# The third chunk's product with w_out as seven block products, in a newly ordered list

## The chip, the cores and the metric

The kernel runs on one core of a Trainium2 chip. The metric is device time in microseconds of one execution; the time before is the median of three runs. The profile is one more execution, recorded by the hardware profiler. In it PE is TensorE (PEld its weight loads), DVE VectorE, ACT ScalarE, POOL GpSimd and SP SyncE, which here issues DMAs only.

## The reference

A causal linear attention with a decay per head, followed by a two-layer network with a leaky activation. Four batches, eight heads, 768 positions, head size 64; the network goes from 512 to 2048 and back to 512 for 3072 tokens.

```python
for b in range(S // 64):                       # blocks of 64 positions
    intra = (q_b @ k_b.T) * Dmask              # Dmask[i, j] = lam ** (i - j) for i >= j, else 0
    out_b = intra @ v_b + (q_b * lam_pow) @ kv_state
    kv_state = lam ** 64 * kv_state + (k_b * rev_pow).T @ v_b
x = out.transpose(0, 2, 1, 3).reshape(3072, 512)
h = x @ w_in                                   # 512 -> 2048
g = max(h, 0) + alpha * min(h, 0)
result = g @ w_out                             # 2048 -> 512, float32
```

## The kernel before, in words

**Chunks and units.** The 3072 tokens are six chunks `c` of 512: two batches (`bi`) times 256 positions. The attention of a chunk is done in four units (`bi`, half of the heads `hh`), numbered 0 to 23, so that unit `n` belongs to chunk `n // 4`. For a unit, `load` and `load16` bring q, k and v into SBUF, `cast` makes fp16 of q and k, `turn` with `turned` (on TensorE and a copy) or `turn_by_dma` (a transposing DMA on SyncE's queue, from unit 8 on) turns them, `key_decayed` and `decayed` scale k and q, and `spread` copies a state into the block layout RD. `cluster(old, new)` is TensorE's part: the scores of unit `new` and its state's update (tiles `s` and `acc`), and the outputs of unit `old`, whose scores `masked` has multiplied by the decay mask on VectorE. `state` carries the state on; `out_of` puts the unit's output into xT.

**The network.** `up(c, f, bi, slot)` multiplies a chunk by one of 16 blocks of 128 columns of w_in, four matmuls into a PSUM bank `slot` (tile `h_ps`); `bi=None` means all 512 tokens. `below` (ScalarE) makes the negative part `m`, `gate` (VectorE) writes G from `m` and `h_ps`. The bank is free for another `up` when its `gate` is done.

**The product with w_out.** There are two forms. Chunks 0 to 2 use `down(c, t, part)`: for each of four row tiles `t` 16 matmuls of 512 columns (tile `o_ps`), in parts of four, then `store`, a copy on ScalarE and a DMA on its queue. Chunks 3 to 5 use seven block products instead of eight: G is cut into rows `e` and block parity `r`, w_out into parity and column half. `product(c, k, bi)` is block product `k` for one half of the tokens, eight matmuls of 256 columns (tile `p_ps`). It needs sums of G's blocks (`SUM`, tile `gsum`; sum 3 is made in G itself) and of w_out's (`WS`, tile `wsum`, made by `weight_sum` and negated by `weight_less`). `taken` collects a product into the output tile (ScalarE copies for 1, 6, 7, 4; VectorE adds for 2, 5, 3), and SyncE stores it. A sum of G is made in halves `h`, either by `gate_sum` (an addition on VectorE or GpSimd) or by `gate_copied` and `gate_added`: a DMA on SyncE that copies the first addend, and a DMA on GpSimd's queue that adds the second one. In the list before, chunk 3 uses the DMAs, chunks 4 and 5 use `gate_sum` on VectorE.

**Order.** The scheduling is manual: every engine and every DMA queue executes its instructions in the order of one long list of calls at the end of the kernel, and waits where data or a buffer is not ready. The list is written out, call by call; its opening is common to both versions. The tables `PRODUCTS`, `WHEN` and the function `sums_in` above the list are not called by it. Buffers come from pools of fixed size (four for raw q, five for raw k, two output tiles), so a load or a first write may wait for the last reader of an older tile. The two G buffers alternate between chunks. `hold` writes one element of a raw tile, which makes a load wait for VectorE's place in the list. `fill` are matmuls whose results are not used.

Of the kernel before, what the change touches and what calls it, by code (L numbers as in the profile page):

```python
# [11 lines left out]
def kernel(  # L12
# [434 lines left out]
    G = {}  # L447
# [67 lines left out]
    SUM = {}  # L515
# [38 lines left out]
    def parts(c, k, h, where="q"):  # L554

        if k != 3 and (c, k) not in SUM:
            SUM[c, k] = late(where, "gsum")
        x = {n: SUM[c, n][:, ds(h * HJ, HJ)] for n in (1, 2, 4) if (c, n) in SUM}
        x[3] = block_of(c, 1, 0, h)
        a, b = {  # L560
            1: lambda: (x[3], block_of(c, 1, 1, h)),
            2: lambda: (block_of(c, 0, 0, h), x.get(1)),
            3: lambda: (x[3], block_of(c, 0, 0, h)),
            4: lambda: (block_of(c, 0, 1, h), x.get(2)),
        }[k]()
        return x[k], a, b

    def gate_sum(c, k, h, where="q", eng="V"):
        x, a, b = parts(c, k, h, where)
        engine(eng).tensor_tensor(out=x, in0=a, in1=b, op=ALU.add)  # L570
# [66 lines left out]
    def weight_less_of(c, k, h):  # L637
        weight_less(h)

    WHEN = {  # L640
        (3, 9): [(gate_copied, 1, 0), (gate_copied, 2, 0)],
        (3, 10): [(gate_added, 1, 0), (gate_added, 3, 0)],
        (3, 12): [(gate_copied, 4, 0)],
        (3, 13): [(gate_added, 2, 0)],
        (3, 14): [(weight_less_of, 2, 0)],
        (4, 0): [(weight_less_of, 2, 1), (gate_copied, 1, 1), (gate_copied, 2, 1), (gate_copied, 4, 1)],
        (4, 1): [(gate_added, 1, 1), (gate_added, 3, 1), (gate_added, 2, 1)],
        (4, 5): [(gate_added, 4, 0)],
        (4, 8): [(gate_added, 4, 1)],
    }  # L650

    def sums_in(x):

        if 17 <= x <= 20:
            for h in range(2):
                weight_sum((1, 2, 4, 3)[x - 17], h)
# [89 lines left out]
    state(1, 0)  # L746
    cast(4, "k", "A")
# [6 lines left out]
    masked(2, 1)  # L754
    turned(3, "A")
# [12 lines left out]
    load_win(3)  # L768
    hold("k", 2, 0)
    masked(3, 0)  # L770
    spread(3, 1, "A", True)
# [3 lines left out]
    cast(6, "q", "G")  # L775
    turn(4)
    turned(4, "V")
    cast(7, "q", "G")
    zeros(2, 0, "G")
    out_of(2, "A")  # L780
    spread(8, 0, "A")
    below(0, 2, 0)
    key_decayed(5, "G")
    fill(14, 0)
    state(3, 1)
    cluster(3, None)
# [19 lines left out]
    hold("k", 1, 1)  # L806
    gate(0, 6, None)
    gate(0, 5, None)
    state(4, 0)
    up(0, 4, None, 1)  # L810
    load("k", 1, 1)
    spread(4, 1, "V")
    below(0, 0, 1)
    up(0, 8, None, 2)
    gate(0, 0, 1)
    cast(5, "q", "V")
    load("k", 2, 0, ring=1)
    state(4, 1)
    up(0, 3, 1, 0)
    below(0, 4, None)  # L820
    load_wout(1)
    turn(5)
    below(0, 8, None)
    gate(0, 4, None)
    gate(0, 8, None)
    up(0, 7, None, 1)
    below(0, 3, 1)
    gate(0, 3, 1)
    masked(4, 1)
    up(0, 1, 1, 2)  # L830
    turned(5, "A")
    below(0, 1, 1)
    below(0, 7, None)
    masked(4, 0)
    load_wout(0)
    decayed(4, "G")
    gate(0, 1, 1)
    gate(0, 7, None)
    up(0, 9, None, 0)
    below(0, 9, None)  # L840
    cluster(4, 5)
    masked(5, 1)
    gate(0, 9, None)
    up(0, 11, None, 2)
    below(0, 11, None)
    gate(0, 11, None)
    state(5, 0)
    cast(6, "k", "G")
    zeros(3, 0)
    state(5, 1)  # L850
    up(0, 14, None, 1)
    load("q", 2, 0, ring=1)
    spread(5, 1, "A")
    below(0, 14, None)
    gate(0, 14, None)
    decayed(5, "G")
    up(0, 12, None, 0)
    up(0, 10, None, 2)
    masked(5, 0)
    below(0, 10, None)  # L860
    turn(6)
    up(0, 15, None, 1)
    out_of(4, "A")
    cluster(5, None)
    key_decayed(6, "G")
    gate(0, 10, None)
    cast(7, "k", "V")
    up(0, 13, None, 2)
    below(0, 12, None)
    turned(6, "V")  # L870
    below(0, 15, None)
    out_of(5, "A")
    turn(7)
    gate(0, 12, None)
    load_wout(2)
    up(1, 0, 0, 0)
    below(0, 13, None)
    cluster(None, 6)
    below(1, 0, 0)
    gate(0, 15, None)  # L880
    down(0, 2, 0, 1)
    gate(1, 0, 0)
    up(1, 2, 0, 0)
    gate(0, 13, None)
    below(1, 2, 0)
    hold("k", 2, 1)
    turned(7, "A")
# [3 lines left out]
    state(6, 0)  # L891
    load_wout(3)
    gate(1, 2, 0)
    decayed(6, "G")
    key_decayed(7, "V")
    below(1, 1, 0)
    gate(1, 1, 0)
    cast(9, "q", "V")
    decayed(7, "V")
    down(0, 1, 0, 0)  # L900
    spread(6, 1, "A")
    cast(9, "k", "V")
    down(0, 1, 1, 2)
    masked(6, 0)
    down(0, 0, 0, 2)
    down(0, 0, 1, 1)
    down(0, 0, 2, 1)
    state(6, 1)
    down(0, 1, 2, 2)
    cluster(6, 7)  # L910
    out_of(6, "A")
    down(0, 0, 3, 1)
    cast(8, "k", "V")
    load("k", 2, 1, ring=1)
    spread(9, 0, "V")
    load16("v", 2, 0)
    state(7, 0)
    cast(8, "q", "V")
    down(0, 2, 2, 2)
    down(0, 2, 3, 2)  # L920
    turn_by_dma(8)
    store(0, 0)
    spread(7, 1, "A")
    key_decayed(8, "G")
    store(0, 2)
    up(1, 3, 0, 2)
    below(1, 3, 0)
    masked(7, 0)
    masked(7, 1)
    state(7, 1)  # L930
    cast(10, "k", "V")
    weight_sum(1, 0)
    cluster(7, 8)
    masked(8, 1)
    key_decayed(9, "G")
    gate(1, 3, 0)
    down(0, 1, 3, 2)
    out_of(7, "A")
    up(1, 4, None, 1)
    turn_by_dma(9)  # L940
    store(0, 1)
    state(8, 0)
    below(1, 4, None)
    decayed(8, "G")
    load("q", 2, 1)
    key_decayed(10, "G")
    masked(8, 0)
    spread(8, 1, "G")
    up(1, 5, None, 0)
    state(8, 1)  # L950
    cluster(8, 9)
    below(1, 5, None)
    load("q", 3, 0)
    cast(11, "k", "V")
    up(1, 0, 1, 2)
    gate(1, 4, None)
    below(1, 0, 1)
    gate(1, 5, None)
    up(1, 1, 1, 1)
    below(1, 1, 1)  # L960
    gate(1, 0, 1)
    cast(10, "q", "A")
    up(1, 6, None, 0)
    cast(11, "q", "V")
    down(0, 3, 0, 2)
    gate(1, 1, 1)
    up(1, 7, None, 1)
    below(1, 6, None)
    load16("v", 3, 0)
    weight_sum(1, 1)  # L970
    down(0, 3, 1, 2)
    below(1, 7, None)
    gate(1, 6, None)
    masked(9, 1)
    load16("v", 2, 1)
    key_decayed(11, "V")
    up(1, 8, None, 0)
    state(9, 0)
    below(1, 8, None)
    down(0, 3, 2, 2)  # L980
    down(0, 3, 3, 2)
    turn_by_dma(10)
    cast(12, "q", "V")
    load("k", 3, 0)
    masked(9, 0)
    gate(1, 8, None)
    up(1, 11, None, 0)
    spread(9, 1, "A")
    decayed(9, "G")
    gate(1, 7, None)  # L990
    turn_by_dma(11)
    out_of(8, "V")
    store(0, 3)
    up(1, 10, None, 1)
    spread(13, 0, "A")
    decayed(10, "V")
    key_decayed(12, "G")
    below(1, 11, None)
    state(9, 1)
    below(1, 10, None)  # L1000
    cast(12, "k", "V")
    up(1, 13, None, 2)
    gate(1, 11, None)
    cluster(9, 10)
# [3 lines left out]
    load("k", 4, 0)  # L1008
    below(1, 9, None)
    up(1, 15, None, 1)  # L1010
    gate(1, 13, None)
    state(10, 0)
    load("k", 3, 1)
    load("q", 4, 0)
    gate(1, 9, None)
    below(1, 15, None)
    up(1, 12, None, 2)
    turn_by_dma(12)
    below(1, 12, None)
    up(1, 14, None, 0)  # L1020
    gate(1, 15, None)
    masked(10, 0)
    out_of(9, "A")
    cast(13, "q", "G")
    down(1, 0, 0, 1)
    below(1, 14, None)
    gate(1, 12, None)
    cast(13, "k", "G")
    down(1, 0, 1)
    decayed(11, "G")  # L1030
    up(1, 2, 1, 2)
    gate(1, 14, None)
    up(1, 3, 1, 0)
    down(1, 0, 2)
    spread(11, 0, "G")
    down(1, 0, 3)
    below(1, 3, 1)
    cast(14, "k", "G")
    key_decayed(13, "G")
    spread(10, 1, "V")  # L1040
    state(10, 1)
    spread(10, 0, "A")
    masked(10, 1)
    cluster(10, 11)
    spread(14, 0, "V")
    load("q", 3, 1)
    key_decayed(15, "G")
    gate(1, 3, 1)
    below(1, 2, 1)
    gate(1, 2, 1)  # L1050
    state(11, 0)
    cast(16, "k", "A")
    masked(11, 0)
    spread(11, 1, "V")
    state(11, 1)
# [36 lines left out]
    cast(17, "q", "G")
    store(1, 1)
# [482 lines left out]
```

## Time and profile before

| | |
|---|---|
| median of three runs | 213.61 us (213.57 to 213.88) |
| the profiled execution | 213.43 us, of which the span from first to last instruction is 211.6 us |
| TensorE busy | 200.9 us, 95% (2286 matmuls) |
| VectorE, ScalarE, GpSimd busy | 168.9, 112.7 and 83.5 us |
| mean granted TensorE clock | 1.00 |
| DMA | 33.54 MB, 158 GB/s over the span |

Busy is the time in which an engine executes; the ends of matmuls are modelled and overlap the next ones. Groups of instructions are named by the line of the kernel, the engine, the operation, the tile written and the tiles read, and the shape; then come the count, the busy time, the mean of one in ns, and the engine's idle time just before them with what ended it. The waits list names who waited for whom: total, times, longest. The chain of work that ended last is followed back from the end of the execution. "Landing" is the time from a DMA's issue to its arrival.

### The profile page before, as it was taken

The page shows a single profiled execution, that of the slowest core. Times are in us where ns is not written, and L with a number is a line of the kernel's source. Part 1 is how long each engine was busy: PE and PEld are TensorE (multiplying, and loading weights), DVE is VectorE, ACT ScalarE, POOL GpSimd, SP SyncE. Part 2 cuts the span into 40 slices and gives each one's busy share as a digit, 9 for nine tenths or more (in the row PEclk, how much of TensorE's full clock was granted, in tenths as well). Part 3 has the DMA queues.
Part 4 walks back from the last instruction along what each step waited for, and adds up shares of the span by engine and source line. Part 5 has one row for each costly group of instructions (what it writes and reads, how often), then busy time and mean ns, then how long its engine had stood idle before and what let it go on. Part 6 is the DMA issues. An engine that isn't in the chain of part 4 may idle for free.

```text
span 211.6 us, 5657 instructions
## 1 busy us (share of the span) xinstructions
PE 200.9 (95%) x2286; PEld 124.6 (59%) x2286; DVE 168.9 (80%) x347; ACT 112.7 (53%) x231; POOL 83.5 (39%) x122
## 2 busy tenths in 40 slices
PE   4798999999999999999999999999999999999992
PEld 4776555555555455455544545556666766766881
DVE  3799799999689994889988969999669778549731
ACT  3998576643647536455755556363464525354320
POOL 8989199170721570987960083213021000000000
PEclk9999999999999999999999999999999999999999
DMA  4999999998999999899999391867273211011213
GB/s 113 275 184 194 198 237 227 246 245 118 276 238 220 314 222 231 247 152 243 135 208 105 121 222 56 156 149 157 41 187 65 99 53 50 2 50 53 74 53 124
DMA packets 62443, 33.54 MB, mean 158 GB/s; under 512 B 34497, under 2 KB 58577, under 8 KB 62417
## 3 DMA queue, kind: packets, MB, share of 16 engines
q0 software_dynamic: 22096, 12.45, 41.1%
q1 hardware_dynamic: 38416, 17.57, 35.8%
q10 hardware_dynamic: 1904, 3.16, 4.4%
q8 instruction: 18, 0.29, 0.6%
q14 instruction: 9, 0.07, 0.1%
HBM read 27.28 MB, written 6.29 MB: 159 GB/s over the span
## 4 chain that ended last, share of the span: by engine, by line
PE 78%; ACT 9%; DVE 6%; DMA 4%; issue 2%; ACTq 0%; DVEq 0%; SPq 0%
PE h_ps L457 36%; PE p_ps L598 17%; PE o_ps L491 15%; PE s L362 3%; DVE g L481 3%; PE acc L374 2%; DMA qkT<-qk 2%; DMA lam_sb<-in_lam_dram 2%; ACT qkT L248 2%; PE acc L344 2%; ACT dmask L202 1%; DVE RD L250 1%; ACT qk L248 1%; PE acc L391 1%; DVE sm L403 1%
## 5 line engine op out<-in xcount | busy, mean ns | idle before, releaser
L457 PE MATMUL h_ps<-xT,w_in_sb 128*128 128x512 f16 (+1 forms) x416 | 92.8, 363 | 1.0 <-DVE g L481 0.6
L468 ACT ACTIVATE m<-h_ps 128x512 f32<-128x512 f32 (+1 forms) x104 | 57.5, 564 | 59.9 <-PE h_ps L457 55.0
L481 DVE SCALAR_TENSOR_TENSOR g<-m,oma,h_ps 128x512 f16<-128x512 f32 (+1 forms) x104 | 71.1, 702 | 19.3 <-ACT m L468 18.2
L457 PEld LDWEIGHTS <-w_in_sb 128*128 128x128 f16 x416 | 39.3, 98 | 38.9 <-issue 1.8
L491 PE MATMUL o_ps<-w_out_sb,g 128*128 128x512 f16 x192 | 45.9, 379 | 0.2 <-DVE g L481 0.2
L403 DVE TENSOR_TENSOR sm<-s,dmask 128x512 f16<-128x512 f32 x48 | 32.1, 684 | 2.2 <-PE s L362 2.1
L491 PEld LDWEIGHTS <-g 128*128 128x128 f16 x192 | 18.2, 98 | 20.7 <-issue 0.2
L321 POOL TENSOR_TENSOR qdT<-qkT,qdecay 128x512 f16<-128x512 f16 (+1 forms) x16 | 17.5, 1096 | 16.8 <-DMA qkT<-qk 13.0
L598 PEld LDWEIGHTS <-g 128*128 128x128 f16 x192 | 18.8, 98 | 4.8
L279 POOL TENSOR_TENSOR kdec<-kraw,kdecay 128x512 f16<-128x512 f32 x13 | 13.7, 1063 | 8.4 <-DMA kraw<-in_k_dram 8.3
L428 DVE SCALAR_TENSOR_TENSOR R<-R,rdecay,acc 128x64 f16<-128x64 f16 x60 | 13.8, 272 | 3.7 <-PE acc L391 1.9
L598 PEld LDWEIGHTS <-gsum 128*128 128x128 f16 x144 | 14.0, 98 | 3.1
L252 POOL COPY RD<-R 64x128 f16<-64x128 f16 x24 | 7.8, 324 | 16.2 <-DVE R L428 15.5
L622 ACT ACTIVATE o_sb<-p_ps 128x512 f32<-128x512 f32 (+1 forms) x16 | 7.6, 489 | 10.8 <-PE p_ps L598 10.8
L248 ACT ACTIVATE xT<-acc 128x512 f16<-128x512 f32 x15 | 8.9, 596 | 8.0 <-PE acc L391 5.4
L238 PE MATMUL op_fill<-ident 128*128 128x128 f16 x109 | 9.3, 253 | 3.0 <-POOL ident masks.py:199 2.7
L598 PE MATMUL p_ps<-wsum,gsum 128*128 128x256 f16 x96 | 12.0, 273 | 0.0
L598 PE MATMUL p_ps<-wsum,g 128*128 128x256 f16 x96 | 11.9, 272 | 0.0
L248 ACT ACTIVATE RD<-R 64x128 f16<-64x128 f16 x28 | 8.6, 306 | 6.1 <-DVE R L428 4.9
L598 PE MATMUL p_ps<-w_out_sb,g 128*128 128x256 f16 x96 | 11.6, 273 | 0.0
L102 POOL DMA_DIRECT2D vh<-in_v_dram x13 | 11.5, 890 | 0.0
L238 PEld LDWEIGHTS <-ident 128*128 128x128 f16 x109 | 8.4, 116 | 3.5 <-POOL ident masks.py:199 2.7
(87 smaller groups left out, 215.4 us busy)
## 6 DMA issues: line engine op xcount, KB each, us to landing
kraw<-in_k_dram SPq DMA_DIRECT2D x8, 512.0 KB, 5.7
out_dram<-o_sb ACTq DMA_DIRECT2D x12, 256.0 KB, 3.1
qraw<-in_q_dram SPq DMA_DIRECT2D x6, 512.0 KB, 7.3
out_dram<-o_sb SPq DMA_DIRECT2D x24, 128.0 KB, 2.0
vh<-in_v_dram POOLq DMA_DIRECT2D x11, 256.0 KB, 6.2
w_in_sb<-in_moe_w_in_dram POOLq DMA_DIRECT2D x4, 512.0 KB, 9.4
w_out_sb<-in_moe_w_out_dram POOLq DMA_DIRECT2D x4, 512.0 KB, 9.5
gsum<-g SPq DMA_DIRECT2D x6, 256.0 KB, 2.6
```

Of the source, the lines that this page charges most:

```text
L102: nc.gpsimd.dma_start(out=rows16(x, c, bi)[:, ds(h0, n), :], in_=source({"q": q, "v": v}[x], c, bi, h0, n))
L238: nc.tensor.matmul(t[:, 0:128], lhsT=ident, rhs=ident, start=True, stop=True)
L248: nc.scalar.activation(out, in_, AF.Copy)
L279: engine(eng).tensor_tensor(out=kdec, in0=kr, in1=d.unsqueeze(3).to_broadcast([128, 2, 4, D]), op=ALU.mult)
L321: engine(eng).tensor_tensor(out=x, in0=y, in1=d.unsqueeze(2).to_broadcast([128, 4, n, 64]), op=ALU.mult)
L403: nc.vector.tensor_tensor(out=t["sm"][hl], in0=t["s"][hl], in1=mask_of(hl, units[n][2]), op=ALU.mult)
L428: nc.vector.scalar_tensor_tensor(out=then[:, hp], in0=R[b, hh, i][:, hp], scalar=rdecay[:, 2 * hh + hp : 2 * hh + hp + 1], in1=kv[:, hp], ...
L457: nc.tensor.matmul(h_ps[:, 0:n] if bi is None else h_ps[:, 0:n].rearrange("p (e j) -> p e j", e=2), lhsT=w_in_sb[:, gi, ts(f, 128)], rhs=x ...
L468: nc.scalar.activation(m[:, 0:n], HP[c, f, bi][:, 0:n], AF.Relu, scale=-1.0)
L481: nc.vector.scalar_tensor_tensor(out=g, in0=mv, scalar=oma[:, f : f + 1], in1=hv, op0=ALU.mult, op1=ALU.add)
L491: nc.tensor.matmul(O[c, t], lhsT=gated(c, f)[:, t // 2, t % 2, :], rhs=w_out_sb[:, f, :], start=(f == 0), stop=(f == NF - 1),)
L598: nc.tensor.matmul(acc, lhsT=lhsT, rhs=rhs, start=(first and j == 0), stop=(j == NJ - 1), skip_group_check=True,)
```

## The change

The third chunk (`c = 2`) no longer calls `down` and `store` but `product` and `taken`, as chunks 3 to 5 do. `SUM` of chunks 2 and 3 for `k = 2` and `4` is no longer a tile of its own but the block of G that is its first addend: the sum is made in place, and its `gate_copied` falls away. Sums of chunk 2 are made partly by VectorE and partly by DMAs; those of chunk 3 by two copies and six adding DMAs, two by VectorE; nine of the sums of chunks 4 and 5 go to GpSimd, as do three weight sums. The tables above the list change, and stay uncalled.

```diff
     def parts(c, k, h, where="q"):
         if k != 3 and (c, k) not in SUM:
-            SUM[c, k] = late(where, "gsum")
+            if where is None and k > 1 and c < 5:
+                SUM[c, k] = G[c][:, int(k == 4), 0].rearrange("p f b j -> p f (b j)")
+            else:
+                SUM[c, k] = late(where or "q", "gsum")
...
-    def gate_sum(c, k, h, where="q", eng="V"):
+    def gate_sum(c, k, h, where=None, eng="V"):
...
-    def gate_copied(c, k, h, where="q"):
+    def gate_copied(c, k, h, where=None):
...
-    def gate_added(c, k, h, where="q"):
+    def gate_added(c, k, h, where=None):
```

The list of calls past the opening is in another order, and many calls name another engine. By count, from before to after: `down` 48 to 32, `product` 44 calls to 60 (half products counted singly), `store` 12 to 8, `taken` 28 to 35, `gate_copied` 6 to 3, `gate_added` 8 to 10; `gate_sum` on VectorE 16 to 13 and on GpSimd 0 to 9; `weight_sum` on VectorE 8 to 5 and on GpSimd 0 to 3. `cast` on VectorE 22 to 10, on ScalarE 10 to 16, on GpSimd 16 to 22; `key_decayed` on VectorE 11 to 7, on GpSimd 13 to 17; `out_of` on VectorE 8 to 6; `turned` on VectorE 2 to 1. One `warm_up` in the middle of the list, an activation that loads a table, is gone. `load("q", 3, 0)` moves from SyncE's queue to GpSimd's (`ring=1`). Places that the prediction speaks of, in the new list:

```diff
+    key_decayed(10, "G")
...
+    load16("v", 2, 1)
...
+    load("q", 3, 0, ring=1)
+    cast(15, "k", "G")
...
+    cast(12, "q", "G")
...
+    key_decayed(13, "G")
...
+    decayed(10, "G")
...
+    load16("v", 3, 0)
+    key_decayed(12, "G")
...
+    cast(15, "q", "G")
...
+    cast(14, "q", "G")
...
+    turn_by_dma(14)
...
+    turn_by_dma(13)
...
+    cluster(12, 13)
...
+    gate_copied(2, 1, 0)
...
+    product(2, 2, 0, "tk", False)
...
+    product(3, 1, 1, 2, False)
...
+    gate_added(3, 2, 0)
...
+    gate_added(3, 2, 1)
...
+    product(3, 6, 0, h=0)
...
+    up(4, 15, None, 1)
+    product(4, 1, 0, 2, False)
...
+    gate_sum(4, 1, 1, "k")
...
+    gate_sum(4, 2, 1, "k", eng="G")
+    gate_sum(4, 3, 1, "k", eng="G")
+    gate_sum(4, 3, 0, "k", eng="G")
...
+    product(4, 6, 0, None, False)
...
+    product(4, 7, 0, None, False)
...
+    gate_sum(5, 3, 1, eng="G")
...
+    product(5, 2, 0, "tk", True)
+    product(5, 4, 1, None, True)
+    taken(5, 2, 0)
+    taken(5, 4, 1)
```

The list before ended with `product(5, 3, 0)` and `product(5, 3, 1)` and four `taken`, the last two of them VectorE's.

More of the change, by code (lines that the diff above doesn't have):

```diff
@@ L858 @@
[L858 to L864, printed above, removed]
-    key_decayed(6, "G")
[L866 to L877, printed above, removed]
+    state(5, 0)
+    up(0, 11, None, 2)
+    up(0, 14, None, 1)
+    masked(5, 0)
@@ L912 @@
[L912 to L921, printed above, removed]
+    turned(7, "A")
+    down(0, 2, 2, 2)
+    down(0, 1, 1, 2)
+    spread(6, 1, "V")
+    state(6, 1)
+    down(0, 0, 0, 2)
+    cluster(6, 7)
+    spread(12, 0, "A")
+    state(7, 0)
+    key_decayed(9, "V")
+    cast(9, "q", "A")
+    down(0, 0, 1, 1)
+    cast(8, "q", "V")
@@ L928 @@
[L928 to L935, printed above, removed]
-    gate(1, 3, 0)
[L937 to L942, printed above, removed]
-    below(1, 4, None)
[L944 to L951, printed above, removed]
+    weight_sum(1, 0, "V")
@@ L973 @@
-    gate(1, 6, None)
+    down(0, 3, 2, 2)
+    gate(1, 7, None)
+    cast(11, "q", "A")
     masked(9, 1)
-    load16("v", 2, 1)
[L976 to L984, printed above, removed]
-    masked(9, 0)
[L986 to L990, printed above, removed]
-    turn_by_dma(11)
-    out_of(8, "V")
@@ L993 @@
[L993 to L999, printed above, removed]
+    out_of(8, "A")
+    below(1, 8, None)
+    down(0, 3, 3, 2)
+    key_decayed(10, "G")
+    cast(14, "k", "A")
+    gate(1, 8, None)
+    spread(9, 1, "A")
+    store(0, 3)
+    key_decayed(11, "V")
+    turn_by_dma(10)
+    load16("v", 2, 1)
+    up(1, 11, None, 0)
+    up(1, 10, None, 1)
+    cast(11, "k", "V")
+    up(1, 13, None, 2)
+    masked(9, 0)
@@ L1213 @@
[L1213 removed]
+    gate_sum(2, 1, 1)
     gate(3, 2, None)
+    cast(20, "k", "A")
+    state(16, 0)
+    up(3, 4, None, 0)
+    key_decayed(19)
     gate(3, 3, None)
[L1216 removed]
+    spread(16, 1, "V")
     below(3, 4, None)
[L1218 to L1219 removed]
+    gate_added(2, 1, 0)
+    gate_sum(2, 3, 0)
+    taken(2, 1, None)
+    up(3, 5, None, 1)
+    cluster(16, 17)
+    load16("v", 5, 1)
+    gate_added(2, 3, 1)
     gate(3, 4, None)
[L1221 to L1222 removed]
@@ L1240 @@
+    gate(3, 6, None)
+    spread(19, 0, "A")
+    taken(2, 2, None)
+    key_decayed(20)
+    up(3, 7, None, 1)
     cast(22, "k", "V")
     up(3, 8, None, 0)
-    cast(20, "q", "A")
+    product(2, 5, 0, "tk", False)
+    below(3, 7, None)
+    gate(3, 7, None)
+    up(3, 9, None, 1)
     below(3, 8, None)
-    down(2, 1, 1)
-    up(3, 9, None, 1)
-    out_of(16)
-    down(2, 1, 2)
+    gate_sum(2, 2, 1)
+    gate(3, 8, None)
+    weight_less(1)
+    product(2, 6, 1, h=0)
+    gate_copied(3, 1, 0)
@@ new lines @@
+    out_of(17, "V")
+    decayed(18)
+    up(3, 14, None, 0)
+    masked(18, 1)
+    below(3, 14, None)
+    up(3, 15, None, 1)
+    below(3, 15, None)
+    turn_by_dma(22)
+    turn_by_dma(20)
+    product(2, 7, 1, None, False)
+    masked(18, 0)
+    turn_by_dma(21)
+    gate(3, 14, None)
+    spread(18, 1)
+    taken(2, 7, None)
+    taken(2, 5, None)
+    cluster(18, 19)
+    key_decayed(21)
+    product(2, 4, 0, None, False)
+    product(2, 4, 1, None, False)
+    state(19, 0)
+    masked(19, 0)
@@ new lines @@
+    product(2, 3, 0, None, False)
+    gate_added(3, 1, 0)
+    out_of(18)
+    spread(19, 1, "V")
+    masked(19, 1)
+    cluster(19, 20)
+    decayed(21, "V")
+    gate_copied(3, 1, 1)
+    gate(3, 15, None)
+    taken(2, 4, None)
+    out_of(19)
+    product(2, 3, 1, None, False)
+    up(4, 1, None, 1)
+    masked(20, 0)
+    up(4, 0, None, 0)
+    decayed(20)
+    below(4, 1, None)
+    state(20, 0)
+    gate_sum(3, 3, 1)
+    product(3, 1, 0, 2, False)
+    masked(20, 1)
+    gate(4, 1, None)
```

978 lines of the change are left out of this document (470 added, 508 removed).

## The prediction

> **What bounds the kernel now.** I read the page's busy shares, slices and engine shares of the chain first.
>
> ```profile
> PE 200.9 (95%) x2286; PEld 124.6 (59%) x2286; DVE 168.9 (80%) x347; ACT 112.7 (53%) x231; POOL 83.5 (39%) x122
> ...
> PE   4798999999999999999999999999999999999992
> ...
> PEclk9999999999999999999999999999999999999999
> ...
> PE 78%; ACT 9%; DVE 6%; DMA 4%; issue 2%; ACTq 0%; DVEq 0%; SPq 0%
> ```
>
> TensorE is at nine tenths or more from the fourth slice to the last but one, at the full granted clock. Then TensorE's own waits:
>
> ```profile
> PE h_ps L457 <- DVE g L481: 0.6, 2, 0.3
> PE acc L391 <- ACT xT L248: 0.5, 1, 0.5
> PE s L362 <- DMA qkT<-qk: 0.4, 1, 0.4
> ...
> PE acc L374 <- issue: 0.3, 1, 0.3
> PE o_ps L491 <- DVE g L481: 0.2, 1, 0.2
> ```
>
> It hardly waited. The rows left out, fills and transposes, belong to the filling of the first 25 us, and asked by windows only 0.8 us (0.4 on `qkT`, 0.2 on a gate twice) lie after 50 us. So from about 20 to 207 us the time is the sum of TensorE's own columns, and another engine matters only where it comes late.
>
> Busy time overstates a pipelined matmul, so the pace comes from unbroken stretches of the chain in order of time (start, length, what):
>
> ```profile
> 44.25 5.18 PE o_ps L491 x24
> ...
> 100.77 4.42 PE h_ps L457 x20
> ...
> 194.60 13.11 PE p_ps L598 x120
> ```
>
> 24 products of 512 columns took 5.18 us, 0.2158 each (and 20 of `up` 0.22); 120 of 256 columns took 13.11 us, 0.1093 each. Half the columns, half the time.
>
> **The exchange.** Chunk 2's `down` is 4 row tiles times 16 blocks, 64 matmuls of 512 columns: 64 x 0.2158 = 13.81 us. Seven block products, twice 8 matmuls each, are 112 of 256 columns: 112 x 0.1093 = 12.24 us. **TensorE gains 1.57 us.** All its other work is the same count in both lists (104 `up`, 28 `cluster`, 8 `turn`, 7 `fill`).
>
> A rule of the Trainium skill speaks against this. "TensorE: Matmul & The Clock Gate", section Back-to-back issue gap, gives a sustained spacing of about 131 ns for 512 columns and 81 ns for 128; on a line between them 256 columns would be 98 ns, an estimate, and the exchange would be 8.4 us against 10.9, a loss of 2.5 us. The 216 and 109 ns of the rows do not agree with it, and the measurement decides.
>
> **Work of the other engines.** Seven products need sums of G and of the weights, and the new list also moves work from VectorE to GpSimd. The groups by line and shape (busy, mean ns | idle before):
>
> ```profile
> L481 DVE SCALAR_TENSOR_TENSOR g<-m,oma,h_ps 128x512 f16<-128x512 f32 x88 | 63.9, 743 | 16.3 <-ACT m L468 15.4
> ...
> L279 DVE TENSOR_TENSOR kdec<-kraw,kdecay 128x512 f16<-128x512 f32 x11 | 8.2, 750 | 0.2 <-ACT kdecay L212 0.2
> L570 DVE TENSOR_TENSOR gsum<-g,gsum 128x1024 f16<-128x1024 f16 x8 | 5.4, 687 | 0.1
> L250 DVE CAST qk<-kraw 128x512 f16<-128x512 f32 x13 | 5.4, 419 | 0.4 <-DMA kraw<-in_k_dram 0.3
> ...
> L250 DVE CAST qk<-qraw 128x512 f16<-128x512 f32 x6 | 4.1, 689 | 0.3 <-DMA qraw<-in_q_dram 0.3
> ...
> L620 DVE TENSOR_TENSOR o_sb<-p_ps,o_sb 128x512 f32<-128x512 f32 x4 | 2.8, 689 | 1.9 <-PE p_ps L598 1.9
> ...
> L468 ACT ACTIVATE m<-h_ps 128x512 f32<-128x512 f32 x88 | 51.6, 597 | 52.4 <-PE h_ps L457 48.6 <-DVE R L428 1.6 <-DVE qk L250 1.1
> ...
> L179 ACT ACT_TABLE_LOAD x1 | 1.3, 1283 | 0.4 <-ACT o_sb L511 0.4
> ...
> L321 POOL TENSOR_TENSOR qdT<-qkT,qdecay 128x512 f16<-128x512 f16 x10 | 12.9, 1293 | 13.4 <-DMA qkT<-qk 13.0
> ...
> L252 POOL COPY RD<-R 64x128 f16<-64x128 f16 x24 | 7.8, 324 | 16.2 <-DVE R L428 15.5
> ...
> L321 POOL TENSOR_TENSOR qdT<-qkT,qdecay 128x256 f16<-128x256 f16 x6 | 4.6, 767 | 3.4 <-DVE qkT L250 2.7 <-ACT qdecay L218 0.6
> ```
>
> VectorE loses 12 casts (6 us at 0.42 to 0.69), 4 key decays (3.0), 3 weight sums and 3 gate sums net (4.1 at 0.687) and three copies (about 2), and gains 3 additions of `taken` (2.1): 13 us less, 169 to 156. ScalarE takes nine casts and copies more (some 6 us at about 0.6) and drops a stray `warm_up` with its table load (1.3 us); its four copies out of chunk 2 stay four. Both stay under 75%.
>
> GpSimd gets 12 sums of 128x1024. None runs there now. Its two-input products take 0.767 us at 256 and 1.293 at 512 columns; on that line 1024 columns are 2.3 us. The floor is VectorE's 0.69; the ceiling comes from the longest product, two rows of 1.826, 3.7:
>
> ```profile
> L321 POOL TENSOR_TENSOR qdT<-qkT,qdecay x16: 671/1158/1826, 11.2 to 123.6; 128x512 f16<-128x512 f16 x10, 128x256 f16<-128x256 f16 x6
> ```
>
> I take 2.3, from the same engine and kind of work. The sums are then 28 us, and with casts and key decays GpSimd comes to about 121 us, 57%. "GPSIMD Engine Reference" of the Trainium skill, section Elementwise — side-by-side cycle accounting, gives about 2.6 cycles an element for two inputs, an estimate of 2.2 us; no run here shows such a sum.
>
> Where could one come late? `gate_sum(4,2,1)`, `(4,3,1)` and `(4,3,0)` stand in a row on GpSimd. The first can start when chunk 4's last gate and VectorE's `gate_sum(4,1,1)` are done: after `up(4,15)` 0.6 for `below`, 0.74 for `gate`, 0.69 for the sum and an estimated 0.3 for what VectorE has queued, 2.3 us. It ends at 4.6, the third at 9.2. TensorE gets to the second half of `product(4,6,0)` after three products, three `up` and half a product, 5.6 us at 0.87 each, and to `product(4,7,0)` after 13 of them, 11.3 us. So 1.0 and 2.1 us are spare, and a sum may cost 3.3 us before TensorE waits; in the tail the last one, `gate_sum(5,3,1)`, has over 3 us by the same count. Cost zero; 0.4 us if a sum took 3.7.
>
> **Sums made in place.** Chunks 2 and 3 add into G itself, so an adding DMA must wait until a product has read the block. The tightest is `gate_added(3,2,0)` behind `product(3,1,1)`; on GpSimd's queue `gate_added(3,2,1)`, `decayed(23)` and `spread(21,1)` stand behind it. The adding DMAs' issue (ns) and landing (us) now:
>
> ```profile
> L578 POOL DMA_DIRECT2D gsum<-gsum x4: 847/856/976, 133.9 to 158.9; - x4
> ...
> DMA to landing us min/median/max: 2.4/3.4/5.3
> ```
>
> Issue 0.9 and landing 3.4 are 4.3 us, 6.2 at the slowest. TensorE has five `up`, two products and a cluster (about 7.1 us) before the product that reads it: 2.8 us spare, 0.9 at the slowest, and `cluster(21,22)`, which needs the spread, comes later. On SyncE `gate_copied(2,1,0)` stands ahead of `turn_by_dma(19)`; its gates are done by then, so it holds nothing. Zero.
>
> **The tail.** VectorE's last row, and ScalarE's copy of the same size:
>
> ```profile
> 207.74 0.76 DVE L620 TENSOR_TENSOR o_sb<-p_ps,o_sb 128x256 f32<-128x256 f32 x2 [2.13 <-PE p_ps L598]
> ```
> ```profile
> L622 ACT ACTIVATE o_sb<-p_ps 128x256 f32<-128x256 f32 x8 | 2.9, 382 | 7.7 <-PE p_ps L598 7.7
> ```
>
> Now two additions (0.76) follow the last product; in the new list one copy (0.38) does, the other result having gone a product earlier. The stores leave one after the other, so of 0.38 I take **0.3 us gained**.
>
> **TensorE's waits in the new order.** The new list makes unit 8's casts earlier, frees VectorE before the gates and drops `warm_up`; it can remove the 0.8 us after 50 us and no more. Before that, stepping `up` against `gate` by the rows above gives waits of 0.2 to 0.3 us where 0.3 and 0.5 stood: zero. Against it stands one long GpSimd chain. SyncE's load of now, `qraw`'s landing, GpSimd's casts, key decays and v loads, the transposes' issue and landing, and the cluster on TensorE:
>
> ```profile
> 52.77 2.05 SPq L89 DMA_DIRECT2D qraw<-in_q_dram  x2
> ...
> DMA to landing us min/median/max: 4.4/7.3/9.4
> ...
> L252 POOL CAST qk<-qraw x7: 602/622/1265, 7.2 to 124.8; 128x512 f16<-128x512 f32 x7
> ...
> L279 POOL TENSOR_TENSOR kdec<-kraw,kdecay x13: 1037/1048/1223, 18.0 to 130.4; 128x512 f16<-128x512 f32 x13
> ...
> L102 POOL DMA_DIRECT2D vh<-in_v_dram x13: 772/902/947, 4.2 to 108.8; - x13
> ...
> L305 SPq DMA_TRANSPOSE qkT<-qk x16: 1232/1258/5396, 50.0 to 154.2; - x16
> ...
> DMA to landing us min/median/max: 3.1/5.0/8.7
> ...
> 89.86 0.39 PE L344 MATMUL acc<-qdT,RD 128*128 128x128 f16 x4
> ```
>
> `load("q",2,1)` goes out at about 52.8, as now, and lands at 60.1. GpSimd does `cast(10,"q")` 0.6, `key_decayed(10)` 1.0, `load16("v",2,1)` 0.9 and then, moved from SyncE's queue to its own, `load("q",3,0)`: issued at 62.6, landed at 69.9. `cast(12,"q")` waits for it, and all of GpSimd's queue behind it: up to `cast(14,"q")` five casts (3.1), three key decays (3.1), two spreads (1.3), a `decayed` (1.2), three v loads (2.7) and a q load (0.9), 12.3 us, to 82.2. SyncE transposes unit 14 and, 1.3 later, unit 13, landed at 88.5. TensorE is due at `cluster(12,13)` at 89.86 now, with the same work ahead of it; less the old waits, 89.1. That is 0.6 us of room by medians; the fastest landings give some 8 us, the slowest landings and issue cost over 10. I put 0.4 us lost here and at other close places against 0.4 us of the old waits gone: zero together, between -0.8 and +10.
>
> **Sum.** The profiled execution ran 213.43 us, 211.6 of it span, 0.18 below the median of 213.61. 213.43 - 1.57 - 0.3 = 211.56, on the median 211.74. As the unknown term can cost more than it can give, I put **211.9**. A measurement of this kernel can tell about 0.2%, 0.43 us, from no change.
>
> **The rivals.** *The GpSimd chain decides (slower).* The place is `cluster(12,13)`. For it: an in-order queue blocked by its own load, the transpose issue of 5.4 us, 0.6 us of room. Against: the loads may leave earlier or land at 4.4, and the clusters behind have two us and more. From 1.9 us of lateness on the change loses. One slow landing (9.4 for 7.3) and one slow issue (5.4 for 1.3) make 2.1 + 4.1 - 0.6 = 5.6 us late, 217.3; half of that gives 214.5. Chance 0.2.
>
> *Small waits eat the gain.* A GpSimd sum of 3.7 us, an in-place add at its slowest, VectorE and GpSimd in each other's way: about 0.4 to 0.9 us each, two of them 1.3 us, 213.0. For it: under 1.1 us of room at four places. Against: a wait moves all later due times back, so they do not add up. Chance 0.12.
>
> *Short products bound by their weight loads (slower).*
>
> ```profile
> L598 PEld LDWEIGHTS <-g 128*128 128x128 f16 x192 | 18.8, 98 | 4.8
> ```
>
> If each paid its 0.098 us beside its columns, 112 x 0.207 = 23.2 us, and the time 223. Against it stand 120 products in 13.11 us. The Trainium skill's spacing, above, belongs here. Chance 0.01.
>
> *The change does not do what it says*: nothing calls its tables WHEN and STEPS, but the list itself calls `product(2,...)` and no `down(2,...)`. Chance 0.
>
> **How the numbers follow.** Forecast 0.67 (211.0 to 212.7), small waits 0.12 (212.7 to 213.6), the chain 0.2, the weight loads 0.01. Below 213.18 lie the forecast and a third of the small waits: faster 0.71. Most of the other small waits are within 0.43 of 213.61: same 0.08. Slower 0.21. The low end is all old waits gone and 0.1 for the tail's other half, 211.74 - 0.8 - 0.1 = 210.8; the high end takes in the small waits and the chain at half its price, 214.7.
>
> **What would show it.** Right: no `o_ps` of chunk 2, 448 `p_ps` instead of 336 at 0.109 us, VectorE near 156 us, GpSimd near 121, ScalarE's copy as the last row, and TensorE's waits after 50 us still about 1 us. Wrong: a wait of TensorE on `qkT` of over 1.9 us between 80 and 95 us, GpSimd sums over 3.3 us, or 256-column products slower than 0.123 us (13.81 / 112), at which the exchange gives nothing.

## The result, and the profile after

Over eleven executions each, the changed kernel ran in 212.28 us at the median (210.70 to 213.66) and the kernel before in 214.09 (213.24 to 214.84). The ratio is 0.9914, 95% interval 0.9885 to 0.9944: 1.8 us faster. On the 213.61 us from which the prediction started, that ratio is 211.8.

In the runs below, some executions were in a disturbed state; the ranges hold them, the ratios leave them out, and the profiles of new_order_down and cast8_later are of such executions.

The profiled execution took 212.89 us (span 211.1), 0.6 above its median. Its page, busy shares, slices and engine shares of the chain:

```profile
PE 199.7 (95%) x2334; PEld 129.7 (61%) x2334; DVE 158.8 (75%) x322; ACT 116.2 (55%) x238; POOL 120.2 (57%) x149
...
PE   4897899989999999999899999999999999999993
...
PEclk9999999999999999999999999999999999999998
...
PE 72%; DMA 12%; ACT 8%; POOL 3%; DVE 2%; issue 1%; DVEq 0%; ACTq 0%
```

TensorE is still the bound at full clock, but a DMA has 12% of the chain where it had 4%, and GpSimd, not in it before, has 3%. The groups by line and shape (busy, mean ns of one | idle before), then the end of the chain (start, length, what):

```profile
L491 PE MATMUL o_ps<-w_out_sb,g 128*128 128x512 f16 x128 | 29.6, 379 | 0.4 <-DVE g L481 0.4
...
L573 POOL TENSOR_TENSOR gsum<-g,gsum 128x1024 f16<-128x1024 f16 x4 | 8.5, 2124 | 12.6 <-DVE gsum L573 12.4
...
L573 DVE TENSOR_TENSOR gsum<-g,gsum 128x1024 f16<-128x1024 f16 x4 | 5.3, 1320 | 0.0
```
```profile
193.51 13.99 PE p_ps L601 x128
207.50 0.02 issue
207.52 0.38 ACT o_sb L625
```

`o_ps` has 128 matmuls instead of 192, and the `p_ps` groups, not all shown, have 448 instead of 336; 128 products of 256 columns in a row took 13.99 us, 0.1093 each; one copy of ScalarE comes last. TensorE's waits after 26 us:

```profile
PE acc L344 <- POOL RD L252: 1.2, 1, 1.2
PE h_ps L457 <- DVE g L481: 0.4, 2, 0.3
PE o_ps L491 <- DVE g L481: 0.4, 1, 0.4
```

None is for `qkT`, and the two longest for a gate lie at 44 and 45 us. The one for RD is `cluster(14,15)`, at 101 us. The chain there in order of time:

```profile
86.79 10.24 DMA qkT<-qk
97.03 0.07 issue
97.10 1.16 POOL qdT L321
98.26 2.08 POOL wsum L545
100.34 0.24 POOL RD L252
...
100.98 0.29 PE acc L344 x2
```

Unit 15's transposing DMA stands on SyncE's queue behind two loads and lands 10.24 us after its issue. GpSimd, which waits for it in `decayed(15)`, then does `weight_sum(4,1)` before `spread(14,1)`, for which the cluster has been waiting since 99.8. VectorE's rows show the other place (start, length, what; in brackets the idle time before):

```profile
43.07 0.43 DVE L250 CAST qk<-kraw 128x512 f16<-128x512 f32 x1 [1.55 <-DMA kraw<-in_k_dram]
43.42 0.74 DVE L481 SCALAR_TENSOR_TENSOR g<-m,oma,h_ps 128x512 f16<-128x512 f32 x1
44.08 0.68 DVE L403 TENSOR_TENSOR sm<-s,dmask 128x512 f16<-128x512 f32 x1
44.68 0.47 DVE L481 SCALAR_TENSOR_TENSOR g<-m,oma,h_ps 128x256 f16<-128x256 f32 x1
```

`cast(8,"k")` waits for k's load, and two gates that free TensorE's banks stand behind it. How far this wait belongs to the kernel and how far to this one execution is taken up under cast8_later.

**Where the time went.** I summed, over each trace, the time from one matmul's start to the next one's by the line of the first. `down` fell from 42.13 to 28.11 us, `product` rose from 36.58 to 48.88: together -1.72. From the last matmul's start to the end it was 4.21 us, now 3.90: -0.31. Against that stand +1.12 on the matmuls with RD (L344, the wait at 101 us), +1.03 on `up` of 256 columns (0.56 of it the gate at 45 us, the rest in the first 30 us), and -0.65 on all the rest. The sum is -0.5, the difference of the two spans (211.65 and 211.11).

### The profile page after: what moved, and what is told of

It reads as the page before. It is cut to its first block, busy times and chain, and to the rows that moved or that the text cites. A ratio compares the mean times of both kernels' runs of the same rounds, so it can differ in the third digit from the quotient of the medians.

```text
span 211.1 us, 5774 instructions
## 1 busy us (share of the span) xinstructions
PE 199.7 (95%) x2334; PEld 129.7 (61%) x2334; DVE 158.8 (75%) x322; ACT 116.2 (55%) x238; POOL 120.2 (57%) x149
## 4 chain that ended last, share of the span: by engine, by line
PE 72%; DMA 12%; ACT 8%; POOL 3%; DVE 2%; issue 1%; DVEq 0%; ACTq 0%
PE h_ps L457 31%; PE p_ps L601 23%; PE o_ps L491 11%; DMA kraw<-in_k_dram 5%; DMA qkT<-qk 5%; PE s L362 2%; PE acc L374 2%; PE acc L344 2%; DMA lam_sb<-in_lam_dram 2%; ACT qkT L248 2%; ACT dmask L202 1%; DVE g L481 1%; POOL wsum L545 1%; ACT qk L248 1%; PE acc L391 1%; POOL qdT L321 1%
## 5 line engine op out<-in xcount | busy, mean ns | idle before, releaser
L601 PEld LDWEIGHTS <-g 128*128 128x128 f16 x320 | 31.0, 98 | 8.0
L491 PE MATMUL o_ps<-w_out_sb,g 128*128 128x512 f16 x128 | 29.6, 379 | 0.4 <-DVE g L481 0.4
L491 PEld LDWEIGHTS <-g 128*128 128x128 f16 x128 | 12.2, 98 | 14.5 <-issue 0.6
L601 PE MATMUL p_ps<-wsum,g 128*128 128x256 f16 x160 | 20.4, 273 | 0.0
L601 PE MATMUL p_ps<-w_out_sb,g 128*128 128x256 f16 x160 | 20.3, 273 | 0.0
L279 POOL TENSOR_TENSOR kdec<-kraw,kdecay 128x512 f16<-128x512 f32 x17 | 18.3, 1076 | 2.9 <-DMA kraw<-in_k_dram 2.5
L625 ACT ACTIVATE o_sb<-p_ps 128x512 f32<-128x512 f32 (+1 forms) x20 | 10.2, 511 | 16.3 <-PE p_ps L601 16.3
L252 POOL COPY RD<-R 64x128 f16<-64x128 f16 x26 | 9.2, 354 | 15.6 <-DVE R L428 10.2
L573 POOL TENSOR_TENSOR gsum<-g,gsum 128x1024 f16<-128x1024 f16 x4 | 8.5, 2124 | 12.6 <-DVE gsum L573 12.4
L248 ACT ACTIVATE xT<-acc 128x512 f16<-128x512 f32 x17 | 10.1, 595 | 7.5 <-DVE R L428 4.2
L601 PEld LDWEIGHTS <-gsum 128*128 128x128 f16 x128 | 12.5, 98 | 2.5
```

The lines of the kernel that those rows point to most:

```text
L248: nc.scalar.activation(out, in_, AF.Copy)
L279: engine(eng).tensor_tensor(out=kdec, in0=kr, in1=d.unsqueeze(3).to_broadcast([128, 2, 4, D]), op=ALU.mult)
L491: nc.tensor.matmul(O[c, t], lhsT=gated(c, f)[:, t // 2, t % 2, :], rhs=w_out_sb[:, f, :], start=(f == 0), stop=(f == NF - 1),)
L601: nc.tensor.matmul(acc, lhsT=lhsT, rhs=rhs, start=(first and j == 0), stop=(j == NJ - 1), skip_group_check=True,)
```

## The experiments

Two theories were to be told apart. **Columns:** the gain is TensorE's fewer columns in chunk 2, and the new order is at best neutral. **Order:** the new order and the moved work bring the gain. A third question was what the two waits cost. Each kernel ran beside the kernel before, whose median was 214.09 to 214.68 us.

| kernel | median, us (range) | ratio to before, 95% interval |
|---|---|---|
| changed kernel | 212.28 (210.70 to 213.66) | 0.9914 (0.9885 to 0.9944) |
| new_order_down | 214.00 (212.48 to 216.00) | 0.9980 (0.9951 to 1.0009) |
| old_order_products | 227.06 (225.97 to 229.81) | 1.0587 (1.0540 to 1.0634) |
| old_order_products_g | 231.66 (229.28 to 232.67) | 1.0774 (1.0707 to 1.0841) |
| old_order_products_units | 228.80 (228.46 to 230.74) | 1.0706 (1.0664 to 1.0748) |
| units_back | 220.47 (219.18 to 232.09) | 1.0278 (1.0242 to 1.0315) |
| spread_first | 211.71 (211.27 to 214.62) | 0.9903 (0.9876 to 0.9931) |
| cast8_later | 211.46 (210.76 to 215.31) | 0.9874 (0.9835 to 0.9913) |
| weight_sums_on_v | 211.89 (211.62 to 212.42) | 0.9872 (0.9837 to 0.9907) |
| gate_sums_on_v | 212.35 (211.95 to 215.74) | 0.9896 (0.9855 to 0.9936) |
| combo1 | 212.03 (211.36 to 213.85) | 0.9896 (0.9846 to 0.9945) |
| combo2 | 211.10 (210.57 to 213.65) | 0.9889 (0.9841 to 0.9938) |
| combo3 | 210.73 (210.59 to 211.66) | 0.9848 (0.9819 to 0.9878) |

### The exchange undone in the new order

```diff
-    product(2, 2, 0, "tk", False)
+    down(2, 0, 0, 2)
...
-    product(2, 1, 0, 2, False)
+    down(2, 0, 1)
...
-    taken(2, 2, None)
+    store(2, 0)
```

> The new list with chunk 2's sixteen product calls replaced, call for call, by its sixteen parts of down (and its sums and taken by four store); all else stays. If the gain is TensorE's columns (112 of 256 against 64 of 512): 1.57 us above the changed kernel, about 213.9 us, with o_ps back at 192 and p_ps back at 336. If the gain comes from the new order and the work moved between engines: as the changed kernel, 212.3. If chunk 2's sums and additions on the other engines cost TensorE time that the columns hide: less than 1 us above it, about 213.

`o_ps` has its 192 matmuls again, and the wait for RD stays:

```profile
L491 PE MATMUL o_ps<-w_out_sb,g 128*128 128x512 f16 x192 | 45.2, 379 | 0.1
```
```profile
PE acc L344 <- POOL RD L252: 1.1, 1, 1.1
```

214.00 us: 1.7 above the changed kernel by the medians, 1.4 by the two ratios (0.0066 of 214.1). By its interval it cannot be told from before. So the order by itself gains nothing that shows, and the exchange has 1.4 to 1.7 of the 1.8 us, the size of the columns. The tail's 0.3 us, which this kernel keeps, is too small to be told from before.

### The exchange alone in the old order

```diff
-    down(2, 0, 0, 2)
+    product(2, 2, 0, "tk", False)
...
     gate(3, 0, None)
+    gate_sum(2, 1, 0)
...
     gate(3, 4, None)
+    weight_sum(4, 0)
+    weight_less(0)
```

> The list of before with only the exchange: chunk 2's sixteen down parts replaced by sixteen product calls, its eight sums on VectorE, the weight sums made earlier. If the columns are the gain: 1.6 us under before, about 212.5, unless VectorE (169 us and some 5 more) now keeps TensorE waiting. If the exchange needs the new order: 214 or more, with TensorE waiting for gates or sums between 105 and 140 us. If the order alone gains: 214.1, as before.

227.06 us, 13 more than before and 14.6 above the expectation of the columns theory. Stretches of before, then the same of this kernel (time; busy us and count of PE, PEld, DVE, ACT, POOL; clock; DMA share; GB/s), and TensorE's longest waits:

```profile
115.00:125.00 10.00, 10.00 (x88) 4.88 (x86) 7.84 (x16) 5.97 (x12) 2.53 (x4) 1.00 0.52 145
125.00:135.00 10.00, 10.00 (x126) 5.35 (x125) 9.19 (x18) 5.82 (x11) 5.15 (x9) 1.00 0.47 109
```
```profile
115.00:125.00 10.00, 7.79 (x80) 4.45 (x80) 9.28 (x18) 3.71 (x6) 0.00 (x0) 1.00 0.12 35
125.00:135.00 10.00, 6.43 (x24) 2.69 (x24) 6.38 (x11) 5.33 (x10) 4.56 (x5) 0.83 0.73 150
```
```profile
PE h_ps L457 <- DVE g L481: 6.3, 10, 2.1
PE s L362 <- DMA qkT<-qk: 2.8, 2, 2.5
```

VectorE has 7.8 to 9.2 of 10 us to do there before, and the sums come on top. Gates come late, and TensorE stands still. In this list the columns' gain is not paid out: the waits cost far more than the 1.6 us that the exchange saves. Two more kernels ask whether it is VectorE's load alone. The first makes the same sums on GpSimd:

```diff
-    gate_sum(2, 1, 0)
+    gate_sum(2, 1, 0, eng="G")
...
-    weight_sum(4, 0)
+    weight_sum(4, 0, "G")
```

> The list of before with only the exchange, as in the run with all sums on VectorE (227.06 us), but chunk 2's eight sums and the four weight sums of k = 3 and 4 on GpSimd. If the exchange failed there because VectorE, busy 9 of 10 us between 105 and 145 us, had no room for some 8 us of sums: most of the 13 us come back, 213 to 216 us. If the place of the products in the list is what matters (their sums are made too shortly before them, on whichever engine): 220 us or more, with TensorE waiting for sums on GpSimd.

231.66 us: worse, though VectorE had none of chunk 2's sums. (The profiled execution, 232.67 us, had 0.93 of the clock on the mean, the least of the four.) Its groups from 105 to 140 us, and the same of before:

```profile
L481 DVE SCALAR_TENSOR_TENSOR g<-m,oma,h_ps 128x512 f16<-128x512 f32 x19 | 13.9, 744 | 4.2 <-ACT m L468 3.6
L250 DVE CAST qk<-kraw 128x512 f16<-128x512 f32 x3 | 6.5, 2194 | 0.0
...
L250 DVE COPY RD<-R 64x128 f16<-64x128 f16 x4 | 3.2, 812 | 0.0
```
```profile
L250 DVE CAST qk<-kraw 128x512 f16<-128x512 f32 x4 | 1.6, 420 | 0.0
```

The casts took 2.19 us each instead of 0.42 while GpSimd was busy without a break (29.8 of 30 us from 105 to 135). The gates, which read PSUM, kept their 0.744. So work sent to GpSimd came back to VectorE as waiting. The second kernel keeps the sums on VectorE and moves other work off it:

```diff
-    key_decayed(21, "V")
+    key_decayed(21, "G")
...
-    decayed(18, "V")
+    decayed(18, "G")
```

> The run of the old list with the exchange and all sums on VectorE (227.06 us), with the same thirty calls on the engines of the new list, so that VectorE has 7.7 us less. If VectorE's load there made the 13 us: 5 us or more come back, 215 to 222. If the order of the calls does it (a sum of the weights that ScalarE's copy waits for, sums just ahead of gates): within 2 us of 227.

228.80 us: nothing came back, against the theory that VectorE's load alone made the 13 us. In that list many of these thirty calls stand behind the stretch from 105 to 125 us, where VectorE still has 9.1 to 9.3 of 10 us. It is also my own insertion that is tried here: another place of the sums in the old list may cost less. That stays open.

### The moved work undone in the new order

```diff
-    cast(20, "k", "A")
+    cast(20, "k", "V")
...
-    key_decayed(21)
+    key_decayed(21, "V")
```

> The changed kernel, same list and products, with thirty calls of units 17 to 23 (casts, key decays, decayed, out_of, spread) back on the engines of the list before: VectorE gets some 7.7 us more between 95 and 155 us, where it works 36.1 of 40 us from 105 to 145. If taking this work off VectorE is what lets the exchange pay: slower by 2 us or more, 214.5 to 219, with TensorE waiting for gates. If only the place of the products and sums in the list matters: 212.3 within 0.5.

220.47 us, 8.2 above the changed kernel, more than I expected. Rows of VectorE, of GpSimd and of TensorE at its longest wait, then TensorE's clock after it:

```profile
115.07 3.10 DVE L250 CAST qk<-kraw 128x512 f16<-128x512 f32 x1
118.09 0.46 DVE L428 SCALAR_TENSOR_TENSOR R<-R,rdecay,acc 128x64 f16<-128x64 f16 x2
118.48 0.73 DVE L481 SCALAR_TENSOR_TENSOR g<-m,oma,h_ps 128x512 f16<-128x512 f32 x1
```
```profile
114.80 0.89 POOL L581 DMA_DIRECT2D g<-g  x1 [2.66 <-DVE gsum L573]
115.40 1.48 POOL L321 TENSOR_TENSOR qdT<-qkT,qdecay 128x512 f16<-128x512 f16 x1
116.52 1.36 POOL L279 TENSOR_TENSOR kdec<-kraw,kdecay 128x512 f16<-128x512 f32 x1
```
```profile
119.27 1.82 PE L457 MATMUL h_ps<-xT,w_in_sb 128*128 128x512 f16 x4 [2.45 <-DVE g L481]
```
```profile
119.00:121.00 2.00, 1.73 (x6) 0.67 (x6) 1.95 (x6) 0.00 (x0) 0.00 (x0) 0.59 0.00 0
121.00:123.00 2.00, 2.00 (x47) 1.60 (x46) 1.54 (x3) 0.60 (x1) 0.00 (x0) 0.56 0.00 0
123.00:126.00 3.00, 3.00 (x22) 1.92 (x21) 1.61 (x3) 1.16 (x4) 1.53 (x2) 1.00 0.04 7
```

`cast(20,"k")`, put back on VectorE, lasts 3.10 us instead of 0.42: it ends 0.3 us after GpSimd's third instruction in a row. The gate behind it comes late, TensorE waits 2.45 us, and over the next four it has 0.59 and 0.56 of its clock, 2 x 0.41 + 2 x 0.44, about 1.7 us, lost. The wait and its aftermath are some 4 of the 8 us. So in the new list the gain is there only with this work off VectorE. Whether the new list with `down` needs that too, no run shows: that it is the exchange that needs it is argued, not shown.

### The wait at 101 us

```diff
+    spread(14, 1, "G")
     decayed(15, "G")
...
-    spread(14, 1, "G")
     cast(19, "k", "G")
```

> The changed kernel with the copy spread(14,1) ahead of decayed(15) on GpSimd, so that it no longer waits for unit 15's transposing DMA and a weight sum. If that chain costs what the trace shows: TensorE's wait of 1.2 us on RD at cluster(14,15) is gone and the time falls by 1.2 to 1.4 us, to about 210.9. If the room is eaten by what is late next: the wait moves to a later cluster or a gate, and the time falls by under 0.5 us.

211.71 us: 0.6 less by the medians, though the intervals overlap. The wait at 101 us is gone. The profiled execution (213.15 us, 1.4 above its median) shows what came in its place, 1.0 us at 107 for `spread(15,1)`, which stands behind `weight_sum(3,1)`, and 1.7 us at 83.6 for VectorE's state. There VectorE and GpSimd had:

```profile
79.10 4.03 DVE L545 TENSOR_TENSOR wsum<-wsum,w_out_sb 128x1024 f16<-128x1024 f16 x1
```
```profile
78.44 0.89 POOL L102 DMA_DIRECT2D vh<-in_v_dram  x1
79.32 1.17 POOL L252 CAST qk<-qraw 128x512 f16<-128x512 f32 x2
80.45 2.12 POOL L545 TENSOR_TENSOR wsum<-wsum,w_out_sb 128x1024 f16<-128x1024 f16 x1
```

VectorE's weight sum, 0.68 us alone, waited through four instructions of GpSimd and ended 0.56 after the last.

The other way is to take the three weight sums off GpSimd, all edited like this one:

```diff
-    weight_sum(4, 1, "G")
+    weight_sum(4, 1, "V")
```

> The changed kernel with its three weight sums of GpSimd on VectorE, same places in the list. If GpSimd's queue costs what the trace shows at cluster(14,15) (spread(14,1) behind a sum of 2.1 us): the wait of 1.2 us goes, no VectorE weight sum takes over 1.2 us, and the time is 211.0 to 211.7. If VectorE's load decides there (2.1 us more between 79 and 103 us): 212.3 or more, with waits for gates or states in the place of the one for RD.

211.89 us. The wait for RD is gone, VectorE's longest weight sum is 1.26 us, and a gate's wait of 0.6 us at 102, behind the sum, takes its place. Both theories had a part of it.

### The wait at 44 us, and the late sums

```diff
-    cast(8, "k", "V")
     gate(0, 13, None)
...
     gate(1, 1, 0)
+    cast(8, "k", "V")
```

> The changed kernel with cast(8,k) on VectorE moved five gates' and masks' lines down, behind gate(1,1,0), so that its wait for k's load (1.55 us at 41.5) does not hold the gates. If that wait costs TensorE what the trace shows: the two gaps of 0.44 and 0.56 us at 44 to 45 us go, time down by 1.0, to about 211.3. If TensorE then only waits later, at cluster(14,15), for DMAs that do not move with it: no change, 212.3, and the wait at cluster(14,15) grows from 1.2 to some 2 us.

211.46 us, 0.8 less by the medians, again with overlapping intervals. That is near the 1.0 us of the two gaps, but that they are the cause is not shown. Five other kernels have the same list up to there: new_order_down, spread_first, weight_sums_on_v, gate_sums_on_v and units_back. In their profiles VectorE waits 0.2 to 0.7 us for this load and not 1.55, and TensorE does not wait at 44 us at all. So the two gaps came with a load that was late in one execution out of six profiled.

The nine sums of chunks 4 and 5 on GpSimd, all edited like this one:

```diff
-    gate_sum(4, 2, 1, "k", eng="G")
+    gate_sum(4, 2, 1, "k")
```

> The changed kernel with the nine sums of chunks 4 and 5 that GpSimd makes back on VectorE, same places in the list. VectorE has 33.8 us of work in the 52 us from 155 us on, and gets 6.2 more. If GpSimd's sums there neither gain nor cost: 212.3 within 0.5. If they are what gives VectorE room at the end: slower by 1 us or more, with TensorE waiting for gates. If VectorE's sums that wait beside GpSimd's (2.27 and 1.63 us instead of 0.69) cost TensorE time: faster by up to 0.5.

212.35 us, no difference. GpSimd's sums of chunks 4 and 5 neither gain nor cost here. VectorE's sums, which had taken up to 2.27 us beside GpSimd's, all took 0.68 to 0.69, and TensorE waited once for one of them, 0.6 us.

### Together

```diff
-    cast(8, "k", "V")
...
     gate(1, 1, 0)
+    cast(8, "k", "V")
...
+    spread(14, 1, "G")
     decayed(15, "G")
...
-    weight_sum(4, 1, "G")
+    weight_sum(4, 1, "V")
```

> The changed kernel with three edits together: cast(8,k) behind gate(1,1,0), spread(14,1) ahead of decayed(15), the three weight sums on VectorE. If the waits at 44 us and at 101 us cost their gaps and nothing takes their place: 1.0 + 1.4 us off, 210.0. If what is late next takes half, as in the runs with one edit each (0.6 and 0.8 us off): 210.9 to 211.3.

212.03 us, above both expectations at the median, 211.4 in three of six executions. The one profiled (211.36) has one wait over 0.3 us after 50 us, 0.9 for the gate behind `weight_sum(4,1)` on VectorE. So that sum went back to GpSimd, now behind `spread(14,1)`. The next kernel has, beside the first two edits:

```diff
-    weight_sum(2, 1, "G")
+    weight_sum(2, 1, "V")
...
-    weight_sum(3, 1, "G")
...
     spread(15, 1, "G")
+    weight_sum(3, 1, "G")
```

> The changed kernel with cast(8,k) behind gate(1,1,0), spread(14,1) ahead of decayed(15), weight_sum(2,1) on VectorE, and weight_sum(3,1) behind spread(15,1) on GpSimd. The waits then gone are those at 44, 101 and 107 us and VectorE's sum of 4.03 us beside GpSimd's. If nothing takes their place: 210.3 to 210.9, no wait of TensorE over 0.5 us after 50 us. If the spread of the opening's DMAs (waits before 50 us) decides: 211.3 to 212.0, with the waits before 50 us.

211.10 us. One wait was left in its profile, 0.8 us at 78 for ScalarE's `store(1,0)`, behind `cast(16,"k")`, which waits for unit 12's tile to be free.

```diff
-    cast(16, "k", "A")
...
     store(1, 2)
+    cast(16, "k", "A")
```

> The run with four edits (211.1 us) and one more: cast(16,k) on ScalarE, which waits 2.31 us for a tile of unit 12 at 74 us and holds two below and a store behind it, moved behind store(1,2). If that is the last wait after 50 us: TensorE's 0.83 us at 78 us go, the profiled span is 208.7 and the median 210.3 to 210.6. If the executions differ by their openings alone: the median stays at 211 with the same spread of some 3 us, and the profile shows no wait over 0.3 us after 50 us.

210.73 us, ratio 0.9848 (0.9819 to 0.9878): faster than the changed kernel too, whose interval just does not touch this one. TensorE's whole list of waits after 26 us:

```profile
PE h_ps L457 <- DVE g L481: 0.2, 1, 0.2
```

So five edits of the list, four moves and a change of engine, bring back about 1.5 us (212.28 - 210.73). How much each of them gives was not separated; the wait for RD at 101 us is the one that stands in the profiles of new_order_down and gate_sums_on_v too (1.1 us each).

## Why the prediction was right, and where it was not

**The exchange: right.** 1.57 us were predicted; the two traces give 1.72 (with 0.4 us of the gap at 44 us counted in `down` after, and older waits in `down` before), the kernel with the exchange undone 1.4 to 1.7. The products went at 0.1093 us each, as in the chunks before them. The trace goes with the formula N/2.4 + 2.5 ns, which section Back-to-back issue gap of "TensorE: Matmul & The Clock Gate" in the Trainium skill keeps for single matmuls (109 and 216 ns), and not with its sustained spacing.

**The tail: right,** 0.31 for 0.3, by the last row. (A slip without consequence: of TensorE's slices before, the fourth is 8 tenths, so that it is at nine from the fifth on.)

**Work of the engines: nearly.** GpSimd had 120.2 us for 121 and its sums 2.12 us for 2.3 (one 2.58). VectorE had 158.8 for 156: of the 2.8 us, 2.5 are two sums of 2.27 and 1.63 us instead of 0.69, each ending 0.5 us after GpSimd's sums beside it. The limit of 3.3 us for a GpSimd sum was read off the first of the three in a row; the third, due at 11.3, allows (11.3 - 2.3) / 3 = 3.0, and at 3.7 us it would have come 2.1 us late, not 0.4. In the room behind the in-place sums the issue is counted twice, as landing is taken from the issue's start: 3.4 us and not 4.3. At the measured times neither slip mattered, and no matmul of `p_ps` waited.

**TensorE's waits: right in the sum, by luck.** I put 0.4 us of new waits against 0.4 of old ones, zero together. On the medians that held: 211.8 by the ratio, 211.74 by the sum. But after 26 us the profile before has 1.2 us of waits and the one after 2.0, of which 0.7 stand at 44 us; the rest, 1.3, is nearly all the wait for RD. Both sides are about three times what I put, and that they balance was not worked out. The profiled execution alone is 1.3 us over the sum (212.89 for 211.56), and the gaps at 44 us, about 1.0 by the starts of the matmuls, are most of that. `cast(8,"k")` in front of two gates I had not followed at all; the opening was settled by stepping `up` against `gate` only.

**The GpSimd chain: right in kind, wrong in place.** `cast(14,"q")` was put at 82.2 and ended at 81.5; unit 13's transposed tile was put at 88.5 and came just before 89.49, when GpSimd's `decayed(13)` began:

```profile
89.49 1.17 POOL L321 TENSOR_TENSOR qdT<-qkT,qdecay 128x512 f16<-128x512 f16 x1 [0.77 <-DMA qkT<-qk]
```

`cluster(12,13)` began at 89.67 and did not wait. It had been due at 89.1; TensorE came 0.6 us later, after the gaps at 44 us, and without that almost nothing of the room would have been left: luck. In the profiles of the five kernels named under cast8_later the tile came 0.2 to 3.5 us before the cluster's scores. The step that failed is "the clusters behind have two us and more": two clusters on, a sum of 2.1 us stood between a late transpose and a copy that TensorE needed, and 1.2 us were lost. That is under the 1.9 us from which the change would lose, so the forecast held.

**Not predicted:** that the same exchange without the new order, or without the work moved off VectorE, ends 6 to 17 us slower than before. The prediction put the moved work at no cost; in the new list the gain is not there without it. My rival "VectorE and GpSimd in each other's way" named the mechanism, at 0.4 to 0.9 us; in units_back one such cast led to some 4 us.

## What to carry to other kernels

A saving on the busiest engine is read off its own columns, but it is paid out only where the other engines have room in that stretch; undo the saving and undo the moved work separately to see both. On an in-order queue, put what the bound engine waits for ahead of long work and of anything that waits for a DMA. Work given to GpSimd is not free for VectorE when VectorE copies or adds from SBUF beside it.

## What the runs showed of the hardware

**VectorE waits for GpSimd over several instructions.** A cast of 0.42 us lasted 3.10, a sum of 0.68 us lasted 4.03, each until 0.3 to 0.6 us after GpSimd's row of instructions ended; the gates, which read PSUM, kept their 0.744. "SBUF — State Buffer" of the Trainium skill, section Who interferes with whom, says that copies and casts can contend with GpSimd, that instructions with two SBUF inputs do where GpSimd reads SBUF, and that the one that issues later waits for the other's instruction; the traces agree, and here the wait went on through three and four instructions.

**A long wait costs more than its length.** After 2.45 us without a matmul TensorE had 0.59 and 0.56 of its clock over stretches of two us; asked for 119.40 to 122.70 us alone, the profile of units_back gives 0.50, and 1.00 from 122.80 on. So it is half the clock for some 3.4 us. The same fall follows waits of 2.06 and 2.54 us in old_order_products, the first with three shorter waits in the five us before it, and one of 1.87 us in old_order_products_g, each time to 0.50. A wait of 1.7 us left it at 1.00:

```profile
82.00:84.00 2.00, 0.43 (x12) 0.33 (x16) 1.51 (x3) 0.48 (x1) 0.57 (x1) 1.00 1.80 195
84.00:86.00 2.00, 2.00 (x55) 1.21 (x56) 1.27 (x4) 0.60 (x1) 0.68 (x1) 1.00 1.04 269
```

(stretches of spread_first). "TensorE: Matmul & The Clock Gate" of the Trainium skill, section What's actually happening, puts the fall to half rate after an idle window of about 3.4 us; here 1.87 to 2.54 us were enough.
